# A fused retention and gated feed-forward kernel: the eighth chunk is transposed on TensorE instead of by DMA

## The chip, the cores and the metric

One NeuronCore of a Trainium2 chip. The time is the device time of one execution in microseconds (us); compared are medians over executions. A profile is one execution recorded by the hardware profiler, with times counted from the start of its span.

## The reference

Retention attention over 8 batches, 8 heads, 576 positions and a head size of 64, then a feed-forward layer with a sigmoid gate over the 4,608 tokens (d_model 512, d_ff 1536):

```python
gamma = 1.0 - 2.0 ** (-5.0 - np.arange(H))
Dmat = np.where(rel >= 0, gamma[:, None, None] ** rel[None], 0.0)    # rel = i - j
attn = np.matmul((q @ k^T / sqrt(D)) * Dmat, v)                      # per batch and head
x = attn.transpose(0, 2, 1, 3).reshape(B * S, H * D)
gate = 1.0 / (1.0 + np.exp(-(x @ w_gate)))
out = (gate * (x @ w_val)) @ w_out
```

## The kernel before

**Chunks.** Each batch's 576 positions are cut into five chunks, four of 128 and one of 64; they are numbered 0 to 39 through all batches, so chunk 5 opens the second batch and chunk 7, the eighth, is its third. Chunks 0 to 3 are done in pairs at the start by functions of their own. For every later chunk s:

- `load(s)`: three DMAs on the SP queue bring k, q and v (L114; 256 KB each, half for a 64-wide chunk).
- `cast_k`, `cast_q`, `cast_v`: POOL multiplies k and q by decay tables and writes them as bf16 into `qk_nat[s % 4]` (L257 four instructions, L267 one), and copies v into `vbd[s % 4]` (L278 four). Block 0 of `qk_nat` holds q, blocks 1 and 2 hold k for the two halves of the chunk.
- `cross(s)`: one DMA transpose (L294), on the SP queue too, turns the twelve 128x128 blocks of `qk_nat` (eight for a 64-wide chunk) into the tile `T`.
- `turn(s, engs)` is the other way to fill `T`: twelve transposing matmuls (L309) into two banks of the pool that the score products use, and two copies out of PSUM (L311): blocks 0 and 1 by the first engine given, block 2 by the second. Before the change it is called for chunks 5 and 4 alone.
- `phase_qk` (scores, L411, eight matmuls, masked by DVE at L413), `phase_st` twice (running state, L444, copied by DVE at L450), `phase_pv` (L430 and L432, copied to `xT` by ACT at L434). `cast_dense` has ACT cast v once more (L288), in two halves for the next chunk.

**Order.** It is written out by hand. The list `order` holds the phases (`st0`, `qk`, `st1`, `pv` for each chunk) and `advance` runs the next one. When the scores of chunk s are run, `casts_to(s + 3)` first issues casts and transposes up to chunk s + 3, and with them the loads of one chunk more. SP takes its DMAs in program order, so around chunk 7 they stand: transpose of 6; loads of 8; transpose of 7; loads of 9; transpose of 8; loads of 10; transpose of 9; loads of 11; transpose of 10.

**Feed-forward.** TensorE fills the time between the phases with it: products `h` (L513) with the gate and value weights, sigmoid on ACT (L529 or L539), product on DVE (L532, L535 or L543), output products `op` and their copy by `store` (L553). The first 512 tokens go through `op_first` (L734). Then come the tokens 512 to 639: products `h`, then the loop of twelve output products at L755 to L758, with phases put between them, which the change touches:

```python
    for fc in range(NFC):
        if fc in (2, 6, 10):
            advance(at + 1)
        nc.tensor.matmul(opp, lhsT=gvs2[fc], rhs=wo_sb[:, fc, :], start=(fc == 0), stop=(fc == NFC - 1))
    store(opp, 512, 2)
```

The three phases are `st1` and `pv` of chunk 6 and `st0` of chunk 7. After it the loop over `BLOCKS` runs the remaining tokens, and the scores of chunk 7 come after the first eight matmuls of the block at 640.

**Buffers.** `T` has four buffers in rotation; `qk_nat` and `vbd` four each; the score pool two PSUM banks; the feed-forward pool three.

Of the kernel before, what the change touches and what calls it, by code (L numbers as in the profile page):

```python
# [16 lines left out]
def kernel(  # L17
# [208 lines left out]
    on_pool, on_act, on_dve = nc.gpsimd.tensor_copy, nc.scalar.copy, nc.vector.tensor_copy  # L226
# [22 lines left out]
    def cast_k(s):  # L249

        b, c = STEPS[s]
        n = width[c]
        k32 = loaded[s][0]
        kn = qk_nat[s % NB][:, 1:3]
        for j in range(n // 64):
            for hh in range(2):
                nc.gpsimd.tensor_tensor(  # L257
                    out=kn[half(hh), j, :, half(hh)], in0=k32[half(j), hh::2, :],
                    in1=ktab[half(j), c, hh::2].unsqueeze(2).to_broadcast([64, M, D]), op=ALU.mult)
        natural["k", s] = kn  # L260

    def cast_q(s):
        b, c = STEPS[s]
        n = width[c]
        q32 = loaded[s][1]
        qs = qk_nat[s % NB][:, 0].rearrange("p m (hh d) -> p (m hh) d", d=D)
        nc.gpsimd.tensor_tensor(out=qs[0:n], in0=q32[0:n],  # L267
                                in1=qtab[0:n, c, :].unsqueeze(2).to_broadcast([n, H, D]), op=ALU.mult)

    def cast_v(s):  # L270

        b, c = STEPS[s]
        n = width[c]
        v32 = loaded[s][2]
        vb = vbd[s % NB]
        for j in range(n // 64):
            for hh in range(2):
                nc.gpsimd.tensor_copy(out=vb[half(hh), j, :, half(hh)], in_=v32[half(j), hh::2, :])  # L278
        natural["vb", s] = vb
# [10 lines left out]
    def cross(s):  # L290

        nb = 1 + width[STEPS[s][1]] // 64
        t = att_pool.tile([P, 3, M, P], BF16, tag="T", name=f"T_{s}", bufs=4)
        nc.sync.dma_start_transpose(out=t[:, 0:nb].rearrange("p j m t -> p (j m) t"),  # L294
                                    in_=qk_nat[s % NB][:, 0:nb].rearrange("p j m d -> p (j m d)"))
        turned["q", s] = t[:, 0]
        turned["k", s] = t[:, 1:3]

    def turn(s, engs):

        nb = 1 + width[STEPS[s][1]] // 64
        t = (att_pool.tile([P, 3, M, P], BF16, tag="T", name=f"T_{s}", bufs=4) if nb == 3
             else osb_pool.tile([P, 2, M, P], BF16, tag="osb", name=f"T_{s}"))
        for b0, eng in zip(range(0, nb, 2), engs):
            n = min(2, nb - b0)
            ps = qk_psum.tile([P, n, M, P], BF16, tag="qk", name=f"Tp_{s}_{b0}")
            for i in range(n):
                for m in range(M):
                    nc.tensor.matmul(ps[:, i, m, :], lhsT=qk_nat[s % NB][:, b0 + i, m, :], rhs=ident,  # L309
                                     is_transpose=True, start=(i == 0 and m == 0), stop=(i == n - 1 and m == M - 1))  # L310
            eng(out=t[:, b0:b0 + n], in_=ps)  # L311
        turned["q", s] = t[:, 0]
        turned["k", s] = t[:, 1:nb]
# [154 lines left out]
    def loads_to(s):  # L468
        while done["ld"] <= min(NS - 1, s):
            load(done["ld"])  # L470
            done["ld"] += 1

    def casts_to(s):
        while done["cast"] <= min(NS - 1, s):
            x = done["cast"]
            loads_to(x + (1 if x < 16 else 2))
            cast_k(x)
            cast_q(x)
            cross(x)
            cast_v(x)  # L480
            done["cast"] += 1

    def run_phase(kind, s):
        if kind == "qk":
            casts_to(7 if s < 6 else s + LEAD_CAST)
            phase_qk(s)
            if s > 5:
                cast_dense(s + 1, 0)
        elif kind == "pv":
            phase_pv(s)  # L490
            if s > 5:
                cast_dense(s + 1, 1)
        else:
            phase_st(s, int(kind[2]))
# [55 lines left out]
    def store(opp, r0, hold, eng=None):  # L550

        ob = osb_pool.tile([P, DM], FP32, tag="osb", name=f"ob_{r0}")
        (eng or on_act)(out=ob, in_=opp)  # L553
        stores.append([hold if r0 >= LATE else 10 ** 6, r0, ob])
# [40 lines left out]
    def advance(end):  # L595
        nonlocal at
        while at < end:
            run_phase(*order[at])
            at += 1
# [106 lines left out]
    done["cast"] = 6  # L706
    loads_to(7)
    casts_to(6)
    at = 0
    advance(at + 1)  # L710
# [5 lines left out]
    def op_first(fcs):  # L716
        for fc in fcs:
            if fc == 1:
                advance(at + 1)
                cast_wo(4, on_dve)  # L720
            if fc == 2:
                cast_wo(5, on_act)
                cast_wo(6, on_dve)
            if fc == 5:
                turn(4, [on_act])
                cast_wo(7, on_dve)
            if fc in (3, 4, 6, 7):
                advance(at + 1)
            if fc == 7:
                casts_to(8)  # L730
            if fc in (9, 11):
                cast_dense(6, (fc - 9) // 2)
            for nb in range(4):
                nc.tensor.matmul(opps[nb], lhsT=gvs[fc][:, nb * P:(nb + 1) * P], rhs=wo_sb[:, fc, :],  # L734
                                 start=(fc == 0), stop=(fc == NFC - 1))
# [17 lines left out]
            advance(at + 1)  # L753
    opp = ffn_bank([P, 512], "op_512")
    for fc in range(NFC):  # L755
        if fc in (2, 6, 10):
            advance(at + 1)
        nc.tensor.matmul(opp, lhsT=gvs2[fc], rhs=wo_sb[:, fc, :], start=(fc == 0), stop=(fc == NFC - 1))  # L758
    store(opp, 512, 2)

# [47 lines left out]
```

## Time and profile before

| | |
|---|---|
| median of 4 executions | 338.21 us (337.74 to 343.86) |
| the profiled execution | 343.86 us, its span 342.1 us |
| TensorE busy | 329.2 us (96%) |
| VectorE (DVE), ScalarE (ACT), GpSimd (POOL) busy | 168.5, 171.5, 184.4 us |
| mean granted TensorE clock | 0.995 |
| DMA transposes `T<-qk_nat` on SP | 34, median 4.7 us from issue to landing |
| bytes moved by DMA | 60.13 MB |

The page of the profile cuts the span into 40 equal slices, each with the busy share of an engine in tenths. A list of waits names the instruction that waited, the one that released it, the sum in us, how often, and the longest. The timeline gives start, duration, engine, line and tiles; in brackets stands how long the engine was idle before and what ended that. A matmul's duration includes the pipeline; what it costs in a stream is the distance from start to start. The start of a DMA on SPq is its issue by the queue; the transfer lands later.

### The profile page before, as it was taken

To read this page: it belongs to the slowest core of one execution; us is meant where nothing else is said; L and a number is where in the kernel's file an instruction comes from. 1 tells how busy PE (TensorE), PEld (TensorE's weight loads), DVE (VectorE), ACT (ScalarE), POOL (GpSimd) and SP (SyncE) were. 2 spreads that over 40 slices of the span, in tenths; PEclk is the share of its full clock that TensorE was granted. 3 is DMA by queue.
4 is the path that set the end of the run, shared out by engine and by line. 5 is a ranking of instruction groups with operands and counts; after the bars stand their busy time and mean duration, and the time that the engine had idled before them with its cause. 6 is when DMAs were issued, how large, how long until landed. Compare 5 with 4: busy or idle time off the path is not lost.

```text
span 342.1 us, 7590 instructions
## 1 busy us (share of the span) xinstructions
PE 329.2 (96%) x2862; PEld 187.9 (55%) x2862; DVE 168.5 (49%) x354; ACT 171.5 (50%) x353; POOL 184.4 (54%) x328
## 2 busy tenths in 40 slices
PE   7899979797999999999999999999999999999996
PEld 3574547576756656656556655544555455544443
DVE  5858634564647536526526625640675155503420
ACT  6664636546554656345455755363654455324321
POOL 7634657877979775784358975590758500000000
PEclk9999999999899999999999999999999999999999
DMA  7999999999999999999939999992996520020002
GB/s 210 315 348 302 208 249 220 181 191 223 195 188 254 213 272 254 201 252 177 178 100 231 185 196 254 177 186 92 221 200 105 136 68 0 2 92 31 2 31 92
DMA packets 169732, 60.13 MB, mean 176 GB/s; under 512 B 151136, under 2 KB 163680, under 8 KB 169696
## 3 DMA queue, kind: packets, MB, share of 16 engines
q1 hardware_dynamic: 169552, 59.59, 83.7%
q8 instruction: 22, 0.36, 0.4%
q14 instruction: 14, 0.11, 0.1%
q10 hardware_dynamic: 144, 0.07, 0.1%
HBM read 37.75 MB, written 9.44 MB: 138 GB/s over the span
## 4 chain that ended last, share of the span: by engine, by line
PE 75%; DMA 17%; POOL 2%; DVE 2%; issue 1%; SPq 1%; ACT 0%; POOLq 0%; DVEq 0%
PE h L513 44%; PE op L581 22%; DMA ld_k<-in_k_dram 5%; DMA T<-qk_nat 4%; DMA ld_g<-in_moe_w_gate_dram 4%; DMA ld_o<-in_moe_w_out_dram 2%; PE qk L411 2%; PE pv L432 2%; PE pv L430 2%; PE st L444 2%; DMA ld_q_pair<-in_q_dram 1%; POOL qk_nat L257 1%; PE op L572 1%; DVE sbd L450 1%; DVE ptp L356 1%
## 5 line engine op out<-in xcount | busy, mean ns | idle before, releaser
L513 PE MATMUL h<-xT,wg_sb 128*128 128x512 bf16 (+3 forms) x584 | 118.4, 326 | 0.3 <-DVE gv L543 0.2
L513 PE MATMUL h<-xT,wv_sb 128*128 128x512 bf16 (+3 forms) x584 | 118.3, 325 | 0.0
L257 POOL TENSOR_TENSOR qk_nat<-ld_k,ktab 64x256 bf16<-64x256 f32 x128 | 78.3, 612 | 55.3 <-PE st L444 30.4
L543 DVE TENSOR_TENSOR gv<-g,h 128x512 bf16<-128x512 bf16 (+1 forms) x106 | 66.4, 626 | 66.7 <-PE h L513 51.8
L539 ACT ACTIVATE g<-h 128x512 bf16<-128x512 f32 (+1 forms) x106 | 58.2, 549 | 73.5 <-PE h L513 65.8
L581 PE MATMUL op<-wo_sb,gv 128*128 128x512 bf16 x360 | 82.8, 379 | 0.0
L513 PEld LDWEIGHTS <-wg_sb 128*128 128x128 bf16 x584 | 51.9, 99 | 37.3 <-issue 0.4
L450 DVE CAST sbd<-st 64x256 bf16<-64x256 f32 x112 | 47.1, 420 | 48.4 <-PE st L444 46.0
L513 PEld LDWEIGHTS <-wv_sb 128*128 128x128 bf16 x584 | 51.1, 98 | 33.0
L278 POOL CAST vbd<-ld_v 64x256 bf16<-64x256 f32 x128 | 51.1, 399 | 14.1 <-PE pv L432 9.2
L581 PEld LDWEIGHTS <-gv 128*128 128x128 bf16 x360 | 33.3, 98 | 35.1
L288 ACT CAST vs<-ld_v 64x256 bf16<-64x256 f32 x112 | 45.1, 403 | 2.0 <-DMA ld_v<-in_v_dram 0.3
L553 ACT COPY ob<-op 128x512 f32<-128x512 f32 x33 | 19.2, 586 | 43.2 <-PE op L581 40.9
L267 POOL TENSOR_TENSOR qk_nat<-ld_q,qtab 128x512 bf16<-128x512 f32 (+1 forms) x36 | 37.5, 1042 | 2.8
L413 DVE TENSOR_TENSOR pt<-qk,tri 128x512 bf16<-128x512 f32 (+1 forms) x36 | 22.6, 629 | 21.1 <-PE qk L411 20.5
L434 ACT CAST xT<-pv 128x512 bf16<-128x512 f32 (+1 forms) x36 | 19.3, 537 | 20.0 <-PE pv L432 19.9
L444 PEld LDWEIGHTS <-qk_nat 128*128 128x128 bf16 x224 | 14.1, 99 | 9.5
L432 PE MATMUL pv<-pt,vbd 128*128 128x64 bf16 x256 | 19.2, 193 | 0.0
L529 ACT ACTIVATE g<-h 128x256 bf16<-128x256 f32 x28 | 10.8, 384 | 15.2 <-PE h L513 11.3
L411 PEld LDWEIGHTS <-T 128*128 128x128 bf16 x256 | 11.8, 98 | 11.9 <-DMA T<-qk_nat 5.4
L432 PEld LDWEIGHTS <-vbd 128*128 128x128 bf16 x256 | 16.2, 98 | 3.8
L430 PE MATMUL pv<-T,sbd 128*128 128x64 bf16 x228 | 18.1, 193 | 0.0
(72 smaller groups left out, 179.1 us busy)
## 6 DMA issues: line engine op xcount, KB each, us to landing
out_dram<-ob SPq DMA_DIRECT2D x35, 256.0 KB, 2.2
ld_k<-in_k_dram SPq DMA_DIRECT2D x28, 256.0 KB, 4.0
ld_q<-in_q_dram SPq DMA_DIRECT2D x28, 256.0 KB, 4.6
ld_v<-in_v_dram SPq DMA_DIRECT2D x27, 256.0 KB, 4.9
ld_g<-in_moe_w_gate_dram SPq DMA_DIRECT2D x12, 256.0 KB, 6.0
ld_v<-in_moe_w_val_dram SPq DMA_DIRECT2D x12, 256.0 KB, 6.0
ld_o<-in_moe_w_out_dram SPq DMA_DIRECT2D x12, 256.0 KB, 4.7
ld_v<-in_v_dram SPq DMA_DIRECT2D x10, 128.0 KB, 3.6
```

The lines of the kernel that those rows point to most:

```text
L257: nc.gpsimd.tensor_tensor(out=kn[half(hh), j, :, half(hh)], in0=k32[half(j), hh::2, :], in1=ktab[half(j), c, hh::2].unsqueeze(2).to_broadc ...
L267: nc.gpsimd.tensor_tensor(out=qs[0:n], in0=q32[0:n], in1=qtab[0:n, c, :].unsqueeze(2).to_broadcast([n, H, D]), op=ALU.mult)
L278: nc.gpsimd.tensor_copy(out=vb[half(hh), j, :, half(hh)], in_=v32[half(j), hh::2, :])
L288: nc.scalar.copy(out=natural["vs", s][half(hh), j], in_=loaded[s][2][half(j), hh::2, :])
L413: nc.vector.tensor_tensor(out=pt[:, :, 0:n].rearrange("p m (j t) -> p m j t", t=64), in0=qkp[:, :, 0:n].rearrange("p m (j t) -> p m j t", ...
L430: nc.tensor.matmul(pvp[:, m, half(j)], lhsT=before[:, m, :], rhs=qT[:, m, half(j)], start=True, stop=False)
L432: nc.tensor.matmul(pvp[:, m, half(j)], lhsT=vb[:, j, m, :], rhs=pt[:, m, half(j)], start=before is None, stop=True)
L450: nc.vector.tensor_copy(out=sb[half(hh), :, half(hh)], in_=st_tiles[b][half(hh)])
L513: nc.tensor.matmul(out, lhsT=w_sb[:, kc, fc * P:(fc + 1) * P], rhs=xT[:, kc, t0 + a:t0 + e], start=(kc == 0), stop=(kc == NKC - 1))
L539: nc.scalar.activation(out=g[:, 0:n], in_=h1[:, 0:n], func=AF.Sigmoid)
L543: nc.vector.tensor_tensor(out=gvs[some[0]][:, a:e], in0=g[:, 0:n], in1=h2[:, 0:n], op=ALU.mult)
L581: nc.tensor.matmul(opp, lhsT=gvs[fc][:, nb * P:(nb + 1) * P], rhs=wo_sb[:, fc, :], start=(fc == 0), stop=(fc == NFC - 1))
```

## The change

```diff
@@ casts_to(s)
             cast_k(x)
             cast_q(x)
-            cross(x)
+            if x != 7:
+                cross(x)
             cast_v(x)
@@ output products of tokens 512 to 639
     for fc in range(NFC):
-        if fc in (2, 6, 10):
+        if fc in (2, 6, 11):
             advance(at + 1)
+        if fc == 9:
+            turn(7, [on_act, on_dve])
         nc.tensor.matmul(opp, lhsT=gvs2[fc], rhs=wo_sb[:, fc, :], start=(fc == 0), stop=(fc == NFC - 1))
```

The DMA transpose of chunk 7 is left out. Its twelve blocks are transposed by matmuls ahead of output product 9 of tokens 512 to 639, and copied out of PSUM by ACT (blocks 0 and 1) and DVE (block 2). The first state product of chunk 7 moves from ahead of output product 10 to ahead of product 11. On SP the loads of chunk 9 now follow those of chunk 8 directly. The tile `T` of chunk 7 is now taken after those of chunks 8 and 9.

## The prediction

> **What bounds the kernel now.** I read the page's slices first. TensorE is busy in nine tenths or more nearly everywhere; the gaps lie in the first quarter. The list of waits names what ends them:
>
> ```profile
> PE   7899979797999999999999999999999999999996
> PE qk L411 <- DMA T<-qk_nat: 4.5, 3, 2.2
> PE op L734 <- DVE wo_sb L229: 1.7, 2, 1.6
> ```
>
> So 4.5 us of TensorE's idle time, in three pieces, is score products (L411) waiting for chunks transposed by DMA. The timeline of TensorE says where; in the chunk order of the planner the three are chunks 7, 8 and 10 (chunk 9, between them, is the four-matmul one at 77.16 and doesn't wait):
>
> ```profile
> 64.53 0.39 PE L513 MATMUL h<-xT,wv_sb 128*128 128x128 bf16 x4
> 66.69 0.41 PE L411 MATMUL qk<-T 128*128 128x64 bf16 x8 [1.77 <-DMA T<-qk_nat]
> ...
> 71.07 0.41 PE L411 MATMUL qk<-T 128*128 128x64 bf16 x8 [0.59 <-DMA T<-qk_nat]
> ...
> 83.90 0.41 PE L411 MATMUL qk<-T 128*128 128x64 bf16 x8 [2.18 <-DMA T<-qk_nat]
> 84.14 0.60 PE L513 MATMUL h<-xT,wg_sb 128*128 128x256 bf16 x4
> 84.58 0.94 PE L513 MATMUL h<-xT,wv_sb 128*128 128x256 bf16 x4
> 85.32 1.06 PE L513 MATMUL h<-xT,wg_sb 128*128 128x256 bf16 x4
> ```
>
> After 83.9 there is no such wait; later transposes land 3.5 us (chunk 11) to 9 us before use, so a gain of a few us made before 84 would be kept to the end. What feeds these waits is on the SP queue and on POOL:
>
> ```profile
> 60.92 3.72 SPq L294 DMA_TRANSPOSE T<-qk_nat  x1
> 64.68 0.65 SPq L114 DMA_DIRECT2D ld_k<-in_k_dram  x1
> 65.42 0.59 SPq L114 DMA_DIRECT2D ld_q<-in_q_dram  x1
> 66.12 0.59 SPq L114 DMA_DIRECT2D ld_v<-in_v_dram  x1
> 66.81 2.18 SPq L294 DMA_TRANSPOSE T<-qk_nat  x1
> 69.08 0.54 SPq L114 DMA_DIRECT2D ld_k<-in_k_dram  x1
> ...
> 62.56 2.64 POOL L257 TENSOR_TENSOR qk_nat<-ld_k,ktab 64x256 bf16<-64x256 f32 x4
> 65.27 1.04 POOL L267 TENSOR_TENSOR qk_nat<-ld_q,qtab 128x512 bf16<-128x512 f32 x1
> ```
>
> Line one is chunk 7's transpose, which holds the queue 3.72 us and lands 5.73 us after its start, at 66.65; the next three are chunk 9's loads, then chunk 8's transpose and chunk 10's first load. The POOL lines are chunk 8's casts, back to back with chunk 7's before them: they end at 66.31, so chunk 8's transpose can't start sooner.
>
> **What is removed.** One DMA transpose: 12 blocks of 128x128 bf16, 0.39 MB. SP gets 3.72 us back, chunk 9's loads can start at about 60.9 instead of 64.68. [...] At the 290 to 300 GB/s of the load-only half-microseconds here, 0.39 MB would be 1.3 us of the DMA engines; the queue row says 3.72 us. The row decides for SP's time. But neither size reaches the end directly, for the next step is gated elsewhere.
>
> **What is added on TensorE.** The rows of chunk 5's turn are exact models:
>
> ```profile
> L309 PE MATMUL Tp<-ident,qk_nat 128*128 128x128 bf16 x20 | 1.4, 219 | 0.0
> L311 ACT COPY T<-Tp 128x1024 bf16<-128x1024 bf16 x2 | 2.0, 1012 | 0.5 <-PE Tp L309 0.5
> L311 DVE COPY T<-Tp 128x512 bf16<-128x512 bf16 x1 | 0.4, 417 | 0.0
> ```
>
> The 219 ns each is a latency; the cost in a stream is start to start. Chunk 5's twelve start at 39.65 and the next instruction at 40.32: 0.67 us. They run ahead of output product 9, at about 63.55 (the pv of chunk 6 ends at 62.90, then three products of 0.216). Their input, chunk 7's q cast, ended at 60.79: 2.76 us of cover, no stall unless TensorE runs ahead by that much. The two score banks that they take were emptied by 61.7 (the chunk 6 mask on DVE), so no bank wait.
>
> **Evictions.** ACT: 1.01 us. Queued ahead of it are xT of chunk 6 (63.11, 0.59) and two vs casts (63.72 to 64.54), so it runs 64.54 to 65.55. Behind it stand the copy of op_512 (0.59), chunk 8's first vs casts (0.82) and the sigmoid of the next block: these end at 66.14, 66.96 and 67.34. In the profile that sigmoid starts at 67.63, so nobody is later. DVE: 0.42 us at 64.2, ahead of chunk 7's first sbd casts, which move from 64.08 to about 64.85 with their state product, one output product and the transposes later; they are used by pv, after the score product, so they are covered.
>
> **The first score product.** By starts, the last block product ahead of it begins at 64.53 and would be followed 0.22 later, at 64.75; with the transposes' 0.67 TensorE arrives at 65.43 (the idle is counted from the modelled end, 64.92: by that, 65.59). The ACT eviction ends at 65.55 and a release takes about 0.1: chunk 7 starts near 65.65 instead of 66.69. Gain there 1.04 us.
>
> **What is late next.** From chunk 7's to chunk 8's point TensorE needs 71.07 - 0.59 - 66.69 = 3.79 us: it arrives at 69.44. Chunk 8's transpose starts at 66.4 instead of 66.81 (POOL ends at 66.31; SP is idle, its loads long issued) and lands, with the same 4.2 us, at 70.6. So 0.45 of the 1.04 us survives. Bounds of its landing: no earlier than 66.4 + 3.1, the shortest landing in the trace (69.5), and no later than now (71.0). Chunk 10's load is issued when that transpose leaves SP, 0.45 us sooner (up to 1.4 if it issues in the 1.24 us minimum); POOL waits 1.40 us for this load now, and 0.30 for chunk 9's, so chunk 10's casts move by 0.45 to 1.7 at most, and its transpose, landing at 83.85 now, by the same 0.45 (taken, since the issue row next to it is 2.18) to 1.7. That landing sets the start of chunk 10's score product, and from there TensorE is the bound: whatever is gained at chunk 7, the end moves only as chunk 10 does. **Sum: 343.86 of the profiled execution (its span 342.1 and 1.76 around it) becomes 343.4.**
>
> **The clock.** Behind the 2.18 us wait TensorE ran at half clock; granted clock is 0.72 over these 6 us, 1.00 in all windows around:
>
> ```profile
> 84.00:90.00 6.00, 6.00 (x59) 4.79 (x59) 3.13 (x7) 2.02 (x5) 4.61 (x9) 0.72 1.23 201
> ```
>
> 6 x 0.28 = 1.7 us lost. [...] The row decides: if chunk 10's wait falls to that of chunk 7 (1.77, after which the clock stayed at 1.00) another 1.7 us is won. In my sum TensorE arrives at chunk 10 0.45 earlier and the chunk lands 0.45 earlier, so the wait and the drop stay.
>
> **From the profiled execution to the median.** It took 343.86; the other three runs 337.74 to 338.55. The waits and the clock drop, 4.54 + 1.7 = 6.2 us, are about as large as this difference of 5.65. Ordinary runs may have little of either. I apply the change of -0.45 to the median: 337.8.
>
> **Rivals.**
> Likeliest, 0.42, the wait moves on: -1.0 to +0.5, about 337.8; nearly all within 0.3% (1.0 us, about what a measurement here can tell from no change).
> Relief passes through, 0.29: with SP and DMA freed, chunk 8's transpose issues in near its minimum and chunk 10 comes 1.0 to 1.7 us sooner; with the clock drop avoided 2.7 to 3.4, up to 4. For it: the DMA engines' busy share is 0.95 or more in every window up to 160 us, and chunk 10's landing of 7.0 us is the longest in the trace, so a backlog may shrink. Against: POOL, not DMA, gates chunk 8. About 336.0.
> The wait isn't there in ordinary runs, 0.29: then TensorE pays the 0.67, plus about 0.2 at chunk 7, because the ACT eviction ends at 65.55, after TensorE's arrival at 65.43. It decides from the point where chunk 7's DMA would land less than 0.9 us after TensorE's arrival (1.77 in the profile), with no wait left at chunks 8 and 10 to absorb it. +0.9, to +1.5 if the ACT queue, 1.01 us longer, also holds back sigmoids. About 339.1. For it: the 5.65 us above. Against: chunk 8 is gated by POOL in any run, so some wait is left to absorb the cost.
> That the turn doesn't replace the DMA can be excluded: in the instruction order of the changed kernel SP has one transpose less, TensorE twelve more, ACT and DVE a copy each. The changed rotation of T buffers is harmless: each is last read more than 5 us before the next transpose into it.
>
> **Chances.** Faster by over 0.3%: 0.29 + 0.03 = 0.32. Slower: most of the third case, 0.21, + 0.03 = 0.24. Within: 0.44. The range leaves out the far end of the second case: 335.8 to 339.6; the likeliest case alone spans 337.2 to 338.7.
>
> **What would show it.** Right: chunk 7's score product waits under 0.3 us, for ACT's T copy; chunk 8's waits about 1 us for its DMA; POOL's gap ahead of chunk 10's k cast stays over 0.9; chunk 10's product near 83.4 with the clock drop behind it. Wrong: chunk 10's wait gone, or the 0.72 window absent (second case); no wait at all before chunk 10 and a later end (third).

## The result: no difference that can be measured

The changed kernel takes **339.51 us** (median of 43 executions, 336.21 to 343.32), the kernel before 338.83 us (64 executions, 336.94 to 343.86). The ratio of the two, 95% interval in brackets, is **0.9998 [0.998, 1.0017]**. Every ratio here leaves out the slow executions, those more than 1.5% above their kernel's fastest (eight of after's), so it need not be the quotient of the two medians, which is 1.002. The spread changed more than the middle: five of after's executions lie below before's fastest, and its upper quarter begins at 341.1 us against 340.1. One kernel's executions lie up to 7 us apart; a single profile therefore shows mechanisms, and the ratios alone show what they are worth.

The profiled execution of after took 339.76 us with a span of 338.0 us, the clock fully granted throughout. From the page, the slices and one DMA row; from the list of waits, the line that answers to the 4.5 us of before:

```profile
PE   7799999988999999999999999999999999999996
PEclk9999999999999999999999999999999999999999
...
q8 instruction: 22, 0.36, 0.5%
```
```profile
PE qk L411 <- DMA T<-qk_nat: 2.3, 2, 1.4
```

Score products wait for DMA transposes in two pieces instead of three, 2.3 us instead of 4.5. (The second slice row and the q8 row are needed further down.) Where the pieces lie, from the timeline of TensorE, with the copy on ACT from the same view of that engine:

```profile
62.76 0.83 PE L309 MATMUL Tp<-ident,qk_nat 128*128 128x128 bf16 x12
63.42 0.59 PE L761 MATMUL op<-wo_sb,gv 128*128 128x512 bf16 x2
...
64.41 0.39 PE L514 MATMUL h<-xT,wv_sb 128*128 128x128 bf16 x4
64.83 0.41 PE L411 MATMUL qk<-T 128*128 128x64 bf16 x8
...
69.48 0.41 PE L411 MATMUL qk<-T 128*128 128x64 bf16 x8 [0.86 <-DMA T<-qk_nat]
...
81.53 0.41 PE L411 MATMUL qk<-T 128*128 128x64 bf16 x8 [1.40 <-DMA T<-qk_nat]
...
63.76 1.01 ACT L311 COPY T<-Tp 128x1024 bf16<-128x1024 bf16 x1
```

The turn costs TensorE 63.42 - 62.76 = 0.66 us from start to start. Chunk 7's scores start at 64.83, right behind ACT's copy (ended 64.77), with 0.2 us between the last block product and them. Chunk 8 waits 0.86 us, chunk 10 1.40. SP and POOL behind that:

```profile
61.47 0.59 SPq L114 DMA_DIRECT2D ld_v<-in_v_dram  x1
65.46 1.45 SPq L294 DMA_TRANSPOSE T<-qk_nat  x1
67.00 0.85 SPq L114 DMA_DIRECT2D ld_k<-in_k_dram  x1
...
64.39 1.04 POOL L267 TENSOR_TENSOR qk_nat<-ld_q,qtab 128x512 bf16<-128x512 f32 x1
...
72.10 2.64 POOL L257 TENSOR_TENSOR qk_nat<-ld_k,ktab 64x256 bf16<-64x256 f32 x4 [1.74 <-PE pv L432]
```

SP has nothing to issue from 62.06 to 65.46: chunk 9's loads are out, and chunk 8's transpose stands still until POOL's q cast ends at 65.43. It then holds SP 1.45 us. Chunk 10's k load follows at 67.00, and POOL stands idle for 1.74 us before its cast at 72.10; the load landed at 72.0, so the release named in the row (pv, long done) isn't the one that came last.

### The profile page after: what moved, and what is told of

The parts are those of the page before. It is cut to its first block, busy times and chain, and to the rows that moved or that the text cites. A ratio compares the mean times of both kernels' runs of the same rounds, so it can differ in the third digit from the quotient of the medians.

```text
span 338.0 us, 7610 instructions
## 1 busy us (share of the span) xinstructions
PE 327.5 (97%) x2874; PEld 187.5 (55%) x2874; DVE 169.1 (50%) x355; ACT 172.6 (51%) x354; POOL 185.0 (55%) x328
## 4 chain that ended last, share of the span: by engine, by line
PE 74%; DMA 14%; POOL 5%; SPq 3%; issue 2%; DVE 1%; ACT 0%; POOLq 0%
PE h L514 44%; PE op L582 22%; DMA ld_g<-in_moe_w_gate_dram 5%; DMA ld_k<-in_k_dram 4%; DMA T<-qk_nat 3%; POOL qk_nat L257 3%; SPq L123 2%; PE qk L411 2%; PE pv L432 2%; DMA ld_o<-in_moe_w_out_dram 2%; PE pv L430 2%; PE st L444 2%; POOL qk_nat L267 1%; POOL vbd L278 1%; PE op L573 1%
## 5 line engine op out<-in xcount | busy, mean ns | idle before, releaser
L430 PEld LDWEIGHTS <-sbd 128*128 128x128 bf16 x228 | 15.8, 98 | 2.6
L411 PEld LDWEIGHTS <-T 128*128 128x128 bf16 x256 | 11.9, 98 | 9.4 <-DMA T<-qk_nat 2.7
```

The source lines that it names most:

```text
L430: nc.tensor.matmul(pvp[:, m, half(j)], lhsT=before[:, m, :], rhs=qT[:, m, half(j)], start=True, stop=False)
```

## Experiments

The expectations speak of four theories. **M** is the wait that moves on, the forecast. **P** is that the turn's own cost eats the gain. **R** is the rival that the relief of SP and the DMA engines passes through. **F** was formed after eight runs and is told in its place. All ratios are to executions of the kernel before on the same chip, taken together with the run's own.

### Before once more, and no transpose of chunk 7 at all

`b_again` is the kernel before, unchanged. `free7` is after without chunk 7's transposes, by DMA or on TensorE; its scores of chunk 7 read chunk 6's tile. It measures what the whole of these transposes is worth:

```diff
         if fc == 9:
-            turn(7, [on_act, on_dve])
+            for nm in "qk":
+                turned[nm, 7] = turned[nm, 6]
```

> The kernel before, once more, for a profile that stands beside the one of after and for the width of an interval of this size. All theories: ratio 1.00. Theory M (the wait moves on): in its profile TensorE waits at the score products of chunk 7 for the DMA transpose, by 1 to 2 us, again at chunk 8 (0.3 to 0.8) and at chunk 10 (over 1 us). Theory P (the turn's own cost eats the gain): the wait at chunk 7 is about 0.7 us or less, no more than the transposes cost, and chunks 8 and 10 wait little. Theory R (relief of SP and DMA is what acts): the transpose of chunk 8 issues and lands later against POOL's q cast of chunk 8 than in the profile of after.

> Leaves out the transposes of chunk 7 altogether (neither DMA nor TensorE); its score products read chunk 6's tile. Bound of what any way of transposing chunk 7 can give. Theory M: the 0.67 us that TensorE saves against after reappear in front of chunk 8 (its wait 0.86 becomes about 1.5 us) and chunk 10 starts as late as in after (wait about 1.4); time within 0.3% of before. Theory P: 0.7 to 1.0 us faster than after, chunk 8's and 10's waits not longer than in after, end earlier by that. Theory R: as fast as M says or faster, with chunk 10 landing over 0.5 us sooner after POOL's q cast of it.

`b_again`: 338.99 us, ratio 0.9985 [0.9959, 1.0012]. `free7`: 338.42 us, ratio **0.9971 [0.9947, 0.9994]**. TensorE's timeline, first of `b_again`:

```profile
65.25 0.41 PE L411 MATMUL qk<-T 128*128 128x64 bf16 x8 [1.56 <-DMA T<-qk_nat]
...
69.19 0.41 PE L411 MATMUL qk<-T 128*128 128x64 bf16 x8 [0.15 <-DMA T<-qk_nat]
...
80.19 0.41 PE L411 MATMUL qk<-T 128*128 128x64 bf16 x8 [0.21 <-DMA T<-qk_nat]
```

then of `free7`, and below it a window of `free7` (stretch, length, busy time of PE, PEld, DVE, ACT and POOL with their counts, granted clock, DMA share, GB/s):

```profile
63.36 0.40 PE L411 MATMUL qk<-T 128*128 128x64 bf16 x8
...
68.05 0.41 PE L411 MATMUL qk<-T 128*128 128x64 bf16 x8 [0.91 <-DMA T<-qk_nat]
...
81.25 0.54 PE L411 MATMUL qk<-T 128*128 128x64 bf16 x8 [2.09 <-DMA T<-qk_nat]
```
```profile
81.00:90.00 9.00, 8.74 (x92) 7.43 (x93) 4.77 (x12) 4.07 (x11) 7.20 (x13) 0.81 1.23 212
```

In `b_again`, an execution 5.4 us shorter than the profiled one of before, chunk 7 still waits 1.56 us, and chunks 8 and 10 hardly at all. Chunk 7's wait is thus no accident of one execution: in the profiles of all kernels that transpose it by DMA it was 1.4 to 2.0 us except one, `b_pad` below, with 1.02. Yet removing it with all its cost is worth 0.29%, about 1.0 us (0.2 to 1.8). That is the ceiling for any other way of transposing chunk 7 with the rest as it is, and the turn's 0.66 us are to be paid out of it. The profile shows how the rest can be lost: waits of 0.91 us at chunk 8, 0.30 at chunk 9 and 2.09 at chunk 10, and lost clock behind them. It is of an execution of 341.16 us, 2.7 above `free7`'s median, so these sizes aren't those of an ordinary one.

From the start of chunk 11's scores to the end, the span has 250.4 to 250.5 us left in thirteen of the fourteen profiles of this document; only `late10`, next, has more. What sets these executions apart therefore lies before that point, and the distance from chunk 6's scores to chunk 11's measures it: 31.30 us in the profile of before, 27.18 in `b_again`, 28.04 in after.

### What a turn costs where nothing is won

`late10` is before, with ten late chunks turned on TensorE right after their first state product, where their DMA would have landed in time anyway.

```diff
+    BY_PE = [20, 21, 22, 23, 25, 26, 27, 28, 30, 31]
...
-            cross(x)
+            if x not in BY_PE:
+                cross(x)
...
             phase_st(s, int(kind[2]))
+            if s in BY_PE and kind == "st0":
+                turn(s, [on_act, on_dve])
```

> Before, with ten later full chunks (20 to 23, 25 to 28, 30, 31), whose DMA transposes land long before their use, turned on TensorE right after their first state product instead of by DMA. No wait can be removed there, so this is the price of a turn. Theories M and P: 10 x 0.67 = 6.7 us slower (2.0%), if the two evictions (1.01 us on ACT, 0.42 on DVE) stay beside TensorE's work; up to 10 x 1.7 = 17 us if each score product waits for the eviction. Theory R: less than 5 us, since DMA and SP have 10 transposes less and the block products run freer.

347.87 us, ratio 1.0243 [1.0202, 1.0284]: 8.2 us for ten, **0.82 us per turn** (0.68 to 0.96). The group of its transposing products, then two rows of its waits:

```profile
L309 PE MATMUL Tp<-ident,qk_nat 128*128 128x128 bf16 x140 | 9.8, 219 | 0.0
```
```profile
PE qk L411 <- ACT T L311: 0.7, 3, 0.2
PE qk L411 <- DVE T L311: 0.6, 1, 0.6
```

140 products are the 20 of before and ten times twelve. Ten times 0.66 us of stream, and at most 1.3 us of waits for the copies, make 7.9 of the 8.2 us. One profile says the same: its stretch from chunk 11's scores to the end is 258.5 us, 8.0 longer than everywhere else. So the price of the prediction holds, with some 0.1 us per turn on top where copies come just late.

### Does the relief of SP and DMA matter?

`dma_kept` is after, with chunk 7's DMA transpose issued as before too, into a tile that nobody reads.

```diff
-        t = att_pool.tile([P, 3, M, P], BF16, tag="T", name=f"T_{s}", bufs=4)
+        t = (consts.tile([P, 3, M, P], BF16, name="T_unused") if s == 7
+             else att_pool.tile([P, 3, M, P], BF16, tag="T", name=f"T_{s}", bufs=4))
...
-            if x != 7:
-                cross(x)
+            cross(x)
```

> After, with the DMA transpose of chunk 7 issued as before as well, into a tile that nobody reads; SP and the DMA engines get no relief, TensorE does the turn. Theory M (POOL's casts gate chunks 8 and 10, so the relief of SP is worth nothing): same as after within 0.3%; chunk 7's score product waits under 0.3 us, and chunk 8's transpose lands within 0.5 us of where it lands in after, counted from the end of POOL's q cast of chunk 8 (after: 4.0 us behind it). Theory R (relief acts): over 1 us slower than after, chunk 8 and chunk 10 landing 1 us later against POOL. Theory P (price equals gain): same as after.

341.01 us, ratio **1.0044 [1.0019, 1.0069]**. A window of all engines:

```profile
81.00:90.00 9.00, 7.24 (x93) 6.60 (x94) 5.22 (x13) 5.15 (x14) 8.17 (x16) 1.00 1.19 212
```

Against after, measured at another time, this is 0.46%, some 1.5 us; the intervals of the two don't overlap. M had put the relief at next to nothing, and was wrong there. By which path the transfer that nobody waits for costs this isn't shown. In the profile POOL waits 3.05 us for chunk 10's k load, which takes 5.8 us to land instead of after's 5.0, but it is issued 7.47 us behind chunk 6's scores, as in after (7.45), and theory F, below, has another reason for a late landing. The window shows another thing: a wait of 2.05 us at chunk 10 and no loss of clock.

### The waits that come next: chunk 10, and POOL's order

Two edits make what stands behind chunk 7 earlier. `a_turn10` and `b_turn10` are after and before with `BY_PE = [10]` in the manner of `late10`. `a_vlate` and `b_vlate` have POOL cast the v of a chunk behind the k and q of the next one, from chunk 7 on:

```diff
-            cast_v(x)
+            for y in ([x] if x < 7 else [] if x == 7 else [x - 1] if x < NS - 1 else [x - 1, x]):
+                cast_v(y)
```

> After, with chunk 10 turned on TensorE as well, right after its first state product. Theory M: chunk 10's landing is the point at which the gain was lost, so now it comes out: chunk 10's wait of 1.4 us falls to 0.3 or less, 0.67 us are paid for the transposes, and the end is 0.5 to 1.0 us earlier than after (ratio to before 0.997), more where the clock would have dropped. Theory P: 0.7 us slower than after, since each turn costs its transposes. Theory R: chunk 11 and later also land sooner by over 1 us.

> Before, with chunk 10 alone turned on TensorE, right after its first state product; chunk 7 by DMA as before. Theory M: in an undisturbed execution of before chunk 10 waits only 0.2 us, because chunk 7's wait has already held TensorE back; so the turn costs 0.67 and saves 0.2: up to 0.5 us slower than before, not faster, while both turns together were faster. Theory P: 0.2 to 0.7 us slower than before, and turning both is then slower still than after. Theory R: faster than before, since chunk 11 and later land sooner.

> After, with the same putting off of POOL's v casts. Theory M: now no wait stands behind the gain at chunk 7, so it reaches the end: 0.9 us faster than before with late v casts (1.56 of wait against 0.67 of transposes), and 1 to 2.2 us faster than after, whose waits at chunks 8 and 10 are 0.86 and 1.40; ratio to before about 0.996. Theory P: no faster than before with late v casts; the wait removed and the transposes cancel wherever the other waits stand. Theory R: no difference to after, since the DMA engines set the landings.

> Before, with POOL's v casts (1.75 us a chunk) put off behind the k and q casts of the next chunk, from chunk 7 on; the DMA transpose of chunk 7 as before. k and q of chunks 8 and 10 are then ready up to 1.75 us sooner. Theory M: the waits at chunks 8 and 10 vanish, but the one at chunk 7 (1.56 us in the repeat's profile) stays, since chunk 7's q cast doesn't move: 0 to 0.6 us faster than before (0.36 is what chunks 8 and 10 wait in the repeat's profile). Theory P: no change, 0.3% at most.

| | on before | on after |
|---|---|---|
| chunk 10 turned | 0.9986 [0.9956, 1.0017] | **0.9966 [0.9944, 0.9989]** |
| v casts later | 1.0003 [0.9974, 1.0033] | **0.9966 [0.994, 0.9993]** |

Neither edit measurably moves the kernel before, where chunk 7 goes on waiting: 1.97 us in `b_turn10`, 1.91 in `b_vlate`. After with either one is about 0.3% below before, which speaks against P; but in each row the two intervals overlap. With the v casts later, chunk 8's q cast on POOL ends 4.67 us after the start of chunk 6's scores instead of 5.88, and chunk 8 doesn't wait at all; chunk 10 still waits 1.61 us in that profile. In `a_turn10` chunks 8 and 9 wait 0.33 and 0.47. The step from `b_vlate` to `a_vlate`, the change itself with chunk 8 out of the way, is 339.71 to 338.83 us by the medians and 0.37% by the ratios, 1.25 us; M expected 0.9. It is a gain of the size that M names, but the intervals of the two just overlap, so it isn't shown beyond doubt.

### The hidden variable: where TensorE's instructions are fetched

After's landings didn't fit: chunk 10's k load took 5.0 us from issue to landing, in `b_again` 3.8. The page's q8 row is a DMA queue of the kind "instruction" that brings 22 packets, 0.36 MB in all and so 16 KB each; in before they come at 62, 72 and 81 us, about one per 10 us here. They are taken for TensorE's own instructions by their number: after has 5,748 matmuls and weight loads, 261 per packet, and `late10`, `b_pad` and `a_pad`, with 96 to 240 instructions more than the kernels they are made from, have 23 packets. The view of DMA by window, with its columns for an issue "KB each, median us to landing", first for after at the issue and then around the packet:

```profile
ld_k<-in_k_dram SPq DMA_DIRECT2D x1, 256.0 KB, 5.0
...
q8 instruction: 1, 0.02, 19.7%
```

and for `b_again`:

```profile
ld_k<-in_k_dram SPq DMA_DIRECT2D x1, 256.0 KB, 3.8
...
q8 instruction: 1, 0.02, 20.5%
```

After's packet comes at 68.9, while the load (67.00 to 72.0) is under way. `b_again`'s comes at 72.0, when the load (66.83 to 70.7) has landed. Over all fourteen profiles with this load (before's, after's and all runs), sorted by that:

| chunk 10's k load | issue to landing, us | profiles |
|---|---|---|
| a packet comes while it is under way | 4.6 to 5.9 | after, `a_turn10`, `dma_kept`, `b_pad`, `a_pad` |
| none does | 3.6 to 4.2 | before, `b_again`, `free7`, `late10`, `b_turn10`, `b_vlate`, `a_vlate`, `a_again`, `a_both` |

Chunk 11's k load sorts in the same way, though other profiles are hit there: 4.6 to 5.1 us in `b_again`, `late10`, `b_vlate`, `b_turn10`, `a_again` and `a_pad`, 3.4 to 3.7 in the other eight. So it is not the kernel that makes the landing late. The same was counted for all k, q and v loads and transposes issued before 165 us, by whether a packet is under way in the first 3 us after the issue: of 41 transfers that are hit in at least three profiles and missed in at least three, 38 land later when hit, by 0.85 us in the median.

Theory F: a fetch delays the load that it meets, and the turn's 24 instructions more on TensorE (a matmul is a weight load and a product: the page counts 2,874 of each in after and 2,862 in before) bring the fetch forward onto chunk 10's load. To move the fetch and nothing else, some of the warm-up products at the kernel's head were exchanged for more and shorter ones, so that the instruction count changes and the time of the warm-up hardly. `a_pad`, shown here, gives after 128 instructions more; `b_pad`, with `fill(6)` and 54 short products, gives before 96 more. `a_again` is after unchanged, `a_both` is after with chunk 10 turned and the v casts later.

```diff
-    fill(12)
+    fill(4)
+    short = ffn_bank([P, 512], "short")
+    for i in range(72):
+        nc.tensor.matmul(short[:, 0:64], lhsT=blank[:, 0:P], rhs=blank[:, 0:64], start=True, stop=True)
```

> After, once more, beside its variants. Theory F (TensorE's own instruction fetch, 16 KB on the DMA engines every 256 instructions or so, delays the load that it falls upon; the turn's 24 instructions bring the fetch forward into the flight of chunk 10's k load): the fetch comes 1 to 3 us after that load's issue, the load lands over 4.8 us after issue (5.0, 5.9, 5.8 us in three kernels so hit, 3.6 to 4.2 in the seven that weren't), POOL waits over 1 us for it, chunk 10 waits over 1 us. Theory M alone (only POOL gates): landing 3.6 to 4.2 us. Ratio to before 1.00 for both.

> After, with 128 more TensorE instructions at the head (8 of the 12 wide idle products replaced by 72 short ones), where TensorE waits for the first loads; the fetches of instructions then fall half a block, about 4 us, earlier relative to the work. Theory F: chunk 10's k load is in flight between two fetches and lands 3.6 to 4.2 us after its issue, POOL casts chunk 10 about 1 us sooner, chunk 10's score product starts about 1 us earlier counted from chunk 6's (after: 21.98 us), and the time is up to 1 us below after unless the fetch hits another load of the chain. Theory M alone: no change of this landing or of the time.

> Before, with 96 more TensorE instructions at the head (6 of the 12 wide idle products replaced by 54 short ones), so that the fetch which falls just behind the landing of chunk 10's k load comes about 3 us earlier, into its flight. Nothing else is changed. Theory F: that load lands 4.8 us or more after issue instead of 3.6 to 4.0, chunk 10's score product waits over 1 us (0.21 in the repeat's profile) and the kernel is about 0.9 us slower than before. Theory M alone: no change.

> After with both of the steps that gave a ratio of 0.9966 alone: chunk 10 turned on TensorE, and POOL's v casts put off behind the next chunk's k and q casts. Theory M: chunk 8 then waits for nothing (late v casts) and chunk 10 neither (turn): 0.4 to 0.6% below before. Theory P (each turn pays for itself and no more): no better than after with late v casts alone, 0.9966.

| | median us | ratio to before |
|---|---|---|
| `a_again` | 339.38 | 1.0001 [0.9974, 1.0028] |
| `a_pad` | 338.75 | 1.0005 [0.998, 1.0031] |
| `b_pad` | 340.11 | **1.0028 [1.0006, 1.0049]** |
| `a_both` | 337.42 | 0.9975 [0.9949, 1.0002] |

In `b_pad` the fetch comes at 67.5. By its DMA view chunk 8's transpose and chunk 10's k load are both under way then, and both are late:

```profile
T<-qk_nat SPq DMA_TRANSPOSE x1, 5.8
...
ld_k<-in_k_dram SPq DMA_DIRECT2D x1, 256.0 KB, 5.1
```

and by TensorE's timeline chunk 8 waits for it (L414 is L411 of the other kernels, three lines lower):

```profile
64.18 0.41 PE L414 MATMUL qk<-T 128*128 128x64 bf16 x8 [1.02 <-DMA T<-qk_nat]
...
70.08 0.41 PE L414 MATMUL qk<-T 128*128 128x64 bf16 x8 [2.11 <-DMA T<-qk_nat]
```

4.5 and 3.8 us were the two landings in `b_again`, and 0.15 us the wait. The wait comes at chunk 8, where F had expected it at chunk 10, and chunk 11 comes 28.23 us after chunk 6 instead of 27.18. A program that computes the same, with 96 more instructions at its head, is slower by 0.28%, where F expected 0.9 us, about that. The loss goes with more loss of clock, too: 14 of its 22 executions had a mean granted clock below 0.998, and 20 of 75 of before; among the others the medians still are 339.33 and 338.74 us. In `a_pad` the fetch comes at 65.5:

```profile
68.47 0.41 PE L414 MATMUL qk<-T 128*128 128x64 bf16 x8 [0.71 <-DMA T<-qk_nat]
...
78.95 0.40 PE L414 MATMUL qk<-T 128*128 128x64 bf16 x8
85.88 0.41 PE L414 MATMUL qk<-T 128*128 128x64 bf16 x8 [0.71 <-DMA T<-qk_nat]
```

Chunk 8's transpose is hit (4.9 us), the k load less (4.6), and chunk 10 comes 20.25 us after chunk 6 instead of 21.98 in after, without a wait. Yet the time isn't measurably shorter. The next packet (72.2) meets chunk 11's k load, chunk 11 waits 0.71 us, and it comes 27.18 us after chunk 6: 0.86 us sooner than in after, and just as in `b_again`. That `a_pad`, with the larger edit at the head, isn't slower also speaks against the head itself as the reason for `b_pad`'s loss.

`a_again` didn't do what F expected. Its load was issued at 64.90 instead of 67.00 and had landed at 68.8, before the packet came at 70.1, and no score product behind chunk 7's waited:

```profile
60.22 0.40 PE L411 MATMUL qk<-T 128*128 128x64 bf16 x8
...
69.13 0.40 PE L411 MATMUL qk<-T 128*128 128x64 bf16 x8
...
79.60 0.40 PE L411 MATMUL qk<-T 128*128 128x64 bf16 x8
```

Chunk 11 comes 25.44 us after chunk 6 there, 1.74 sooner than in `b_again`, though the end only 0.6, since chunk 6 itself came later; here the wait did not move on. POOL was further ahead of TensorE in it, with chunk 8's q cast ending 3.12 us after chunk 6's scores instead of 5.88. So how far POOL is ahead, and where the loads stand against the fetch, differ between two executions of the same program.

So F is right in this: transfers that a packet of instructions meets landed later, by 0.85 us in the median of the 41 that were counted, and moving the packets cost 0.28% in `b_pad`. That it is why the change brings nothing isn't shown: how often after's executions are hit can't be read from two profiles. That stays open. `a_both` has no wait of a score product for DMA in its profile; its median is the lowest here, but its interval reaches 1.0002. `a_turn10` and `a_vlate` are 0.34% below before, with intervals just short of 1, while before repeated gave 0.9985 itself; which of the three is best can't be told.

## Why the prediction was right, and where it wasn't

**The case and the time.** No difference was forecast as likeliest, and it came. The mechanism named, the wait that moves on, is what one of after's two profiles shows; in the other, `a_again`, no wait came back. So the forecast of the mean is right, and that it comes about by the moving wait in every execution is not. The sizes that the runs measured add up to the same: about 1.0 us for chunk 7's wait with all its cost (`free7`), less 0.66 to 0.82 for the turn, leaves 0.2 to 0.3, less than can be told here. The median, 339.51, lies inside the range by 0.1 us, which is luck; 337.8 was set from three of four executions that were on the low side (before's median over 64 is 338.83). The change, -0.12% forecast, is -0.02% [-0.2, +0.17]. Where the prediction put the decision, at chunk 10 with TensorE the bound from there, is borne out by the constant 250.4 us behind chunk 11.

**TensorE's price:** 0.67 forecast, 0.66 measured in the profile, and 0.82 with everything in `late10`.

**Chunk 7:** under 0.3 us of wait, for ACT's copy: 0.2; the scores start 0.06 us behind the copy's end, where about 0.1 was taken. Chunk 6's scores start at 59.55 in after and at 60.33 in before, so this execution is 0.78 us ahead of the forecast's clock from the outset. Counted from there, chunk 7's scores come after 5.28 us (forecast 65.65 - 60.33 = 5.32), and ACT's copy starts at 63.76 where 64.54 - 0.78 = 63.76 was forecast.

**Chunk 8:** gated by POOL's q cast, about 1 us of wait: 0.86, and its transpose landed 4.0 us after issue where 4.2 was taken. `a_vlate` shows that POOL was the gate. The lower bound was misread: the 3.1 us landing (and the 1.24 us on SP) belong to chunk 39, which has eight blocks; the shortest landing of twelve in that trace is 3.67.

**The price of SP's time** was mis-sized: chunk 8's transpose held SP 1.45 us, not 2.18, which let chunk 10's load out earlier. **The step that failed** is the next: "chunk 10's casts move by 0.45". Counted from chunk 6's scores, the load is issued after 7.45 us instead of 8.75, but lands after 12.45 instead of 12.4, since it takes 5.0 us instead of 3.6. That landing was read as fixed; in the fourteen profiles it is 4.6 to 5.9 us with a packet of instructions under way and 3.6 to 4.2 without. POOL's gap ahead of the cast, forecast as over 0.9 us, is 1.74. Chunk 10's scores come 21.98 us after chunk 6's, forecast 83.4 - 60.33 = 23.07: their transpose landed 5.6 us after its issue instead of 7.0, as it does in `b_again` too (5.1), where the distance is 21.08. So after's chunk 10 is 1.6 us ahead of the profile of before (23.57), and 0.9 behind the ordinary execution `b_again`. Whether the fetch meets the load in most executions is what stays open.

**"Neither size reaches the end directly"**, said of SP's and the DMA engines' relief, was wrong: `dma_kept` puts it at about 1.5 us. It pays for the turn: with the transfer kept, the same change loses 0.44%. The rival of the relief that passes through had the right size for it and the wrong sum. One of its arguments was overstated: in windows of 10 us the DMA engines' share of before up to 160 us is 0.83 in the first and 0.93 from 30 to 40.

**The clock** drop, forecast as a sign behind chunk 10 in after, is absent from its profile, where the wait is 1.40 us: a miss. But it wasn't peculiar to the one execution of before. The profile of `b_vlate`, of 338.89 us and so 0.8 below its median, has it behind chunk 7's wait of 1.91 us:

```profile
64.00:70.00 6.00, 5.04 (x77) 5.04 (x78) 2.57 (x8) 2.38 (x6) 5.14 (x11) 0.72 1.11 212
```

The granted clock was below 0.998 in 13 of after's 44 listed executions, whose median is 2.6 us above that of the others, and in 52 of 181 of before (1.3 to 2.1 us above). So both kernels lose clock in about three executions of ten; where in the span, only profiles could tell.

**The rival without a wait** had a false premise: chunk 7 waits in ordinary executions as well. That chunks 8 and 10 wait little there (0.15 and 0.21 us) it had right.

## What to carry to other kernels

Before a wait is removed, look for the gate of the next piece in the same pipeline: here POOL's casts are released by other things than the transfer that was taken out, and of a wait of 1.4 to 2.0 us only about 1 us could be won. A kernel that leaves the disputed work out altogether gives the ceiling in one run; here 0.29%, with 0.66 us to be paid out of it. A profile of a second execution of the same kernel is worth as much: here it showed the opposite of the first. With nothing changed but the instruction count, 96 more at the head, the packet near chunk 10's k load came at 67.5 us (`b_pad`) instead of 72.0 (`b_again`), and the time was 0.28% longer. So where loads land as closely as here, a change of some tenths of a per cent needs a companion that changes the instruction count alone.

## What the runs showed of the hardware

- A 16 KB packet of the queue of instructions goes with 4.6 to 5.9 us of landing for chunk 10's 256 KB k load when it comes while the load is under way, and 3.6 to 4.2 when none does. In `b_pad` 96 instructions more at the head went with a packet at 67.5 us, a landing of 5.1 us and a kernel slower by 0.28%.
- Waits of 2.18 us (before), 2.09 (`free7`) and 1.91 (`b_vlate`) were followed by a loss of clock: the granted clock was 0.50 from 84.70 to 88.09 in before, 0.81 over the window from 81 to 90 in `free7` and 0.72 over that from 64 to 70 in `b_vlate`, about 1.7 us lost in each. Waits of 1.97 us (`b_turn10`, mean clock 0.999 over its span), 2.05 (`dma_kept`, 1.00 from 81 to 90) and 2.11 (`b_pad`, 1.00 from 70 to 76) weren't. The length of the wait alone doesn't decide at this size.
- A transpose of 0.39 MB held SP for 1.45 us (chunk 8's in after, DMA share 0.33 from 64 to 66.5) and for 3.72 us (chunk 7's in before, DMA share 1.06 to 1.28 from 60.5 to 62). So its size alone doesn't set what it takes from the queue; that the traffic around it does is an estimate from these shares, and no run here tests it.
